# A third pair of exp blocks per unit on VectorE, in units 55 to 62 of a fused state-space and attention kernel

## The chip, the core and the metric

The kernel runs on one core of a Trainium2 chip. The metric is device time in microseconds from launch to end, as the median of several runs. TensorE is called PE below, VectorE DVE, ScalarE ACT, GpSimd POOL; SP is the engine whose queue issues the DMAs. PE multiplies matrices into PSUM (eight banks of 128 x 512 float32), the other engines read PSUM or on-chip memory (SBUF).

## The reference

From x (2048 tokens x 1024) two branches are computed and mixed by a gate of one number per token:

```python
g = sigmoid((x * gate_w).sum(-1, keepdims=True))
a = state_space(x)      # Bu = x B^T (complex), h_t = Lam_bar * h_{t-1} + Bu_t, y = 2 Re(h C^T) + x * Dskip
b = attention(x)        # 32 heads of 32: softmax(q k^T / sqrt(32)) v, then @ wo
out = g * a + (1 - g) * b
```

The attention needs 32 x 2048 x 2048 exponentials. They are what this text is about.

## The kernel before, in words

**Units and bursts.** The 32 heads are taken as 8 groups of 4 heads (`GROUPS`), the 2048 queries as 8 blocks of 256 (`QUNITS`). A group with a block of queries is a unit (0 to 63), and a unit is cut into 8 bursts (`BURSTS`), one for each 256 keys; burst p = 8U + i is burst i of unit U, and there are 512. In this text b0 to b7 are the bursts of a unit. A burst (`burst`, L1615) is 8 score matmuls (L1627, called QK here) into two of three PSUM slots of two banks, then two exponentials, one of each slot, by ACT into bfloat16 tiles: exp(0) at L1646, and exp(1) at L1646 or L1643. The slots rotate (`sl`), so the QK of burst p+1 needs the slot that exp(0) of burst p has read. It is issued as one operation that waits for both of its slots.

**Values.** `pv` (L1732) multiplies the exponentials with V into one PSUM bank (bank 6, token "O"). It runs one burst behind: at burst p it takes exp(1) of burst p-2 and exp(0) of burst p-1, at b1 only what is left of the unit before, at b2 six quarters of a burst at once. After b1 of the next unit the sum over keys is complete: `normalize` issues a reciprocal (L1745) and a multiplication (L1746) on DVE, and a transposing DMA on SP into `OT`.

**The blocks that DVE takes (x).** In chosen bursts ACT's exp(1) leaves out the last 256 of its 1024 columns (L1643 in place of L1646), and DVE and POOL compute these 256 by a polynomial. A pair of such blocks is a batch: two `x_in` (L1636, one in each of the two bursts) scale the scores out of PSUM into integers `xi` (two buffers, by the batch's parity). Then three DVE operations on the 512 columns of both (`x_q`: L1670, L1671, L1667) and one of POOL (`x_p`, L1668) follow, and four small matmuls (`x_pv`, L1711, pvx here) add the batch's values to bank 6. exp(1) of such a burst has an explicit dependence on its `x_in`. There is one `xq` (float32, written by the DVE steps, read by POOL) and one `xp` (bfloat16, written by POOL, read by pvx). So a batch's first `x_q` waits until POOL has read the last batch's `xq`, and POOL waits until the pvx of the last batch is through.

```python
        return [(0.61, DEP, lambda: self.dve(... lo, E2 / E3 * w, lo, ...), i2, ["xq"], "x_q")),      # L1670
                (0.61, DEP, lambda: self.dve(... xq[:], E1 / E3 * w * w, lo, ...), ["xq"] + i2, ["xq"], "x_q")),   # L1671
                (X_LAST, DEP, last)]       # last(): x_q at L1667 on DVE, then x_p at L1668 on POOL
```

**Which bursts.** `X_PLAN` lists half units; in units 55 to 62 both halves are in it, so `X_AT` gives the pairs (b0, b2) and (b4, b6). `x_plan` notes when the values of a batch are taken: at b7 of the unit if the second burst is below 4, else at burst 9, which is b1 of the next unit.

**The order of the work is planned when the program is built.** `build` walks through the bursts with a clock of its own for DVE (`dve_t`) and for the burst (`t0`, advanced by `period`: 1.83, or 1.66 where the burst before has a narrowed exp). In each burst it issues QK, `x_in` (0.40 on its clock, not before t0 + 0.45), exp(0), then `values()` (pv, pvx, exp(1)), the normalization where one is due (0.62 from t0 + 0.86), matmuls of other work ("dense" chains in bank 7, four of 512 columns a burst), and then as much DVE work as fits before `limit`: `period` + 0.86 for a burst in which no chain ends, plus 0.25 before a burst with a normalization; 1.41 + 0.35 where a chain ends and the dense part was put ahead of the values ("behind"); `period` + 0.10 where it ends without that. An `x_q` costs 0.61 (the last 0.615) and 0.12 more (`DEP`) when it follows another x step. Where a chain ends, its evacuation from bank 7 by DVE (0.65 on the clock) is issued after that. The last `x_q` of a batch may not be issued before the pvx of the batch before it. If a batch isn't finished when its values are due, `values()` issues the rest first (`x_flush`). Engines run their queues in order, so this order is what they execute, however long things take.

**Other work in units 55 to 62.** The dense chains are output products (`d_out`, L1538): from unit 55's sixth burst on to burst 511 each takes two bursts, four matmuls in the even burst, four (three in units 55 to 57) in the odd one, and DVE evacuates it at the end of the odd burst with one operation (L1550); unit 55 begins with projections (L1429, evacuated at L1436). The even burst's four matmuls need bank 7 evacuated. Four chains of units 56 and 57 also leave two small DVE steps (L1556, L1557) after two of them.

Of the kernel before, what the change touches and what calls it, by code (L numbers as in the profile page):

```python
# [934 lines left out]

X_AT = ((0, 2), (4, 6), (0, 4))
X_PLAN = (64, 72, 80, 84, 88, 92, 96, 100, 104, 108, 112, 116, 120, 124, 128, 132, 136, 144, 152, 156, 160, 164, 168, 172, 176, 180, 184, 188, 192, 200, 208, 216, 220, 224, 228, 232, 236, 240, 244, 248, 252, 256, 260, 264, 268, 272, 276, 280, 284, 288, 292, 296, 300, 304, 308, 312, 316, 320, 324, 328, 332, 336, 344, 348, 352, 356, 360, 364, 368, 372, 376, 380, 384, 388, 392, 396, 400, 404, 408, 412, 416, 420, 424, 428, 432, 436, 440, 444, 448, 452, 456, 460, 464, 468, 472, 476, 480, 484, 488, 492, 496, 500, 504)
X_COLS = 256
F_TS, F_ST = 1.32, 1.24
DEP = 0.12  # L940
# [22 lines left out]
class FastPath:  # L963

    def __init__(self, nc, S, es, d, flag):
# [27 lines left out]
        self.tq = T("tq", [128, 2, 512], BF)  # L993
        self.xi = T("xi", [128, 2, 2 * X_COLS], I32)
        self.xq = T("xq", [128, 2 * X_COLS], F32)
        self.xp = T("xp", [128, 2 * X_COLS], BF)
        self.ut = T("ut", [128, 2, 512], F32)
# [617 lines left out]
    def burst(self, B):  # L1615
# [17 lines left out]
        if mine is not None:  # L1633
            b, n = mine
            s = sl[1]
            first = self.dve(lambda e: e.tensor_scalar(self.xi[:, b % 2, X_COLS * n:X_COLS * (n + 1)], ps[:, 2 * s + 1, 512 - X_COLS:512], X_A, X_LO, ALU.mult, ALU.max),  # L1636
                             [("S", s)], [("xi", b % 2, n)], "x_in")
        def exp(z):
            s, p = sl[z], self.pt_of(B, z)
            self.pt_own[p] = (B, z)  # L1640
            if z == 1 and first is not None:
                flat = lambda ap: ap.rearrange("p h n -> p (h n)")[:, 0:1024 - X_COLS]
                self.S.op("act", lambda e: e.activation(flat(self.tile[p]), flat(ps[:, 2 * s:2 * s + 2, :]), ACT.Exp, scale=SCALE),  # L1643
# [3 lines left out]
        exp(0)  # L1647
        return lambda: exp(1)

    def x_plan(self, U, pair):  # L1650
        self.x_when.setdefault(8 * U + (7 if pair[1] < 4 else 9), []).append(len(self.x_batch))
        for n, i in enumerate(pair):
            self.x_of[8 * U + i] = (len(self.x_batch), n)
        self.x_batch.append([8 * U + i for i in pair])
# [44 lines left out]
    def x_pv(self, b):  # L1699
# [3 lines left out]
        for n, B in enumerate(self.x_batch[b]):  # L1703
# [3 lines left out]
            def mm(e, n=n, i=i, g=g):  # L1707
                m = None
                for qt in range(2):
                    o = 33 * (4 * qt + 3)  # L1710
                    m = e.matmul(ps[:, 6, o:o + 33], self.xp[:, X_COLS * n + 128 * qt:X_COLS * n + 128 * (qt + 1)], V[:, g % 2, 2 * i + 1, 3, :],  # L1711
                                 start=False, stop=False, skip_group_check=True)
# [44 lines left out]
    def build(self):  # L1757
# [11 lines left out]
        self.plan()  # L1769
        self.pt_own = {}  # L1770
        self.x_of, self.x_batch, self.x_when = {}, [], {}
        self.xbg, self.x_done, self.x_out = [], set(), 0
        self.lane = ""
        self.opening()

# [38 lines left out]
        for p in range(first, NBURST):  # L1814
# [2 lines left out]
            self.p = p  # L1817
            if p > first:
                t0 += period
            if p % 4 == 0 and p in X_PLAN:  # L1820
                one = p % 8 == 0 and p + 4 not in X_PLAN and p < NBURST - 8
                self.x_plan(p // 8, X_AT[2 if one else p // 4 % 2])
            while p in self.x_of and self.x_of[p][1] == 0 and len(self.xbg) > 3:
# [3 lines left out]
            if p in self.x_of:  # L1827
                self.dve_t = max(self.dve_t, t0 + 0.45) + 0.4
                b, n = self.x_of[p]
                if n == 1:  # L1830
                    due = 8 * (p // 8) + (7 if p % 8 < 4 else 9)
                    self.xbg += [(c, d, f, due) for c, d, f in self.x_ops(b)]
                self.lane = "x"
            q0, q1 = self.quarters[p]
# [96 lines left out]
            while self.xbg or self.bg or self.bg2:  # L1931
                now = max(self.dve_t, t0 + 0.3)
                room = limit - now + 1e-9
                xs, bs = [], []
                for c, d, f, due in self.xbg:
                    if c == X_LAST and self.x_out != len(self.x_done):
                        break
                    xs.append((c, d))
                    if c == X_LAST:
                        break  # L1940
                for c, d, f, n in self.bg:
                    if not ((n in self.tabled or not self.bg2) and self.item_ready(n)) or sum(x[0] for x in bs) > room:
                        break
                    bs.append((c, d))
                ts = [(c, 0.0) for c, f in self.bg2[:8]]
                if not bs and not xs and not ts:
                    break
                best = None
                left = next((n for n, x in enumerate(self.xbg) if x[0] == X_LAST), 0) + 1
                soon = self.xbg and left > self.xbg[0][3] - p - X_LEFT  # L1950
                self.hurry = soon and self.xbg[0][3] - p <= 1
                for i in range(len(xs) + 1):
                    for j in range(len(bs) + 1):
                        if self.mixed(xs[:i], bs[:j], [])[0] > room:
                            break
                        for k in range(len(ts) + 1):
                            u, lead = self.mixed(xs[:i], bs[:j], ts[:k])
                            if u > room:
                                break
                            w = sum(x[0] for x in xs[:i] + bs[:j] + ts[:k])  # L1960
                            v = (w + ((0.3 if ended is not None else 9.0) if soon else X_SOON) * i + 0.05 * sum(x[0] for x in bs[:j]), i, j, k, lead)
                            if best is None or v > best:
                                best = v
                lead = best[4]
                if not lead:
                    break
                if lead == "x":
                    c, d, f, due = self.xbg.pop(0)
                elif lead == "b":
                    c, d, f, n = self.bg.pop(0)  # L1970
                else:
                    (c, f), d = self.bg2.pop(0), 0.0
                f()
                if c > 0:
                    self.dve_t = now + c + (d if self.lane == lead else 0.0)
                    self.lane = lead
# [185 lines left out]
```

## Time and profile before

| | us |
|---|---|
| median of 3 runs (lowest, highest) | 923.47 (923.18, 923.78) |
| the profiled execution's own time | 923.41 |
| its span, first to last instruction | 921.6 |
| ACT busy | 903.7 (98%) |
| PE busy | 881.4 (96%) |
| DVE busy | 769.4 (83%) |
| POOL busy | 101.9 (11%) |
| start of unit 55 to start of unit 63 in the span (QK of their b0) | 788.22 to 898.73 |

The profile page lists busy time by engine, the span in 40 slices, the chain of work that ended last, and groups of instructions by line. A busy PE is not a PE at its peak, because the ends of matmuls are modelled. Some matmul records are missing from the trace: of each chain of output products one is mostly not shown. In the timeline a row of "x3" is three instructions in a row on that engine; what stands in brackets is the engine's idle time before it and what ended it. An ACTIVATE's duration overlaps the next one, so the cost of one in a row of them is the distance between starts.

### The profile page before, as it was taken

The page shows a single profiled execution, that of the slowest core. Times are in us where ns is not written, and L with a number is a line of the kernel's source. Part 1 is how long each engine was busy: PE and PEld are TensorE (multiplying, and loading weights), DVE is VectorE, ACT ScalarE, POOL GpSimd, SP SyncE. Part 2 cuts the span into 40 slices and gives each one's busy share as a digit, 9 for nine tenths or more (in the row PEclk, how much of TensorE's full clock was granted, in tenths as well). Part 3 has the DMA queues.
Part 4 walks back from the last instruction along what each step waited for, and adds up shares of the span by engine and source line. Part 5 has one row for each costly group of instructions (what it writes and reads, how often), then busy time and mean ns, then how long its engine had stood idle before and what let it go on. Part 6 is the DMA issues. An engine that isn't in the chain of part 4 may idle for free.

```text
span 921.6 us, 33844 instructions
## 1 busy us (share of the span) xinstructions
PE 881.4 (96%) x15095; PEld 503.7 (55%) x15316; DVE 769.4 (83%) x1365; ACT 903.7 (98%) x1034; POOL 101.9 (11%) x167
## 2 busy tenths in 40 slices
PE   7899998999999999999999999999999999999996
PEld 4555744557545565556655565555655556545553
DVE  2778989999889999999999989999999655676665
ACT  6999999999999999999999999999999999999997
POOL 2000001102101111111111111011110101001000
PEclk9999999999999999999999999999999999999998
DMA  9549767740463202361022420612002114434322
GB/s 202 80 103 154 106 111 138 143 90 16 91 126 90 65 20 61 91 137 45 19 74 65 104 57 19 139 47 83 23 17 54 31 51 134 119 88 123 118 64 75
DMA packets 170983, 77.70 MB, mean 84 GB/s; under 512 B 147280, under 2 KB 155472, under 8 KB 170832
## 3 DMA queue, kind: packets, MB, share of 16 engines
q1 hardware_dynamic: 168672, 74.94, 35.7%
q8 instruction: 121, 1.98, 0.9%
q10 hardware_dynamic: 2160, 0.53, 0.3%
q14 instruction: 30, 0.25, 0.1%
HBM read 25.18 MB, written 20.97 MB: 50 GB/s over the span
## 4 chain that ended last, share of the span: by engine, by line
PE 52%; ACT 28%; DVE 14%; issue 2%; SPq 1%; DMA 1%; POOL 0%
ACT f_pt L1646 22%; PE f_ps L1732 12%; PE f_ps L1627 10%; PE f_ps L1429 8%; PE f_ps L1507 8%; PE f_ps L1460 7%; PE f_ps L1448 5%; ACT f_pt L1643 5%; DVE f_xi L1636 3%; DVE f_ht L1365 2%; SPq L1065 1%; ACT f_cT L1646 1%; DVE f_Ag L1520 1%; DVE f_ub L1464 1%; DVE f_xq L1670 1%
## 5 line engine op out<-in xcount | busy, mean ns | idle before, releaser
L1646 ACT ACTIVATE f_pt<-f_ps 128x1024 bf16<-128x1024 f32 x738 | 712.0, 1082 | 3.3 <-PE f_ps L1627 3.0
L1732 PEld LDWEIGHTS f_ps<-f_V,f_pt 128*128 128x128 bf16 x7140 | 221.7, 96 | 94.8 <-issue 66.3
L1732 PE MATMUL f_ps<-f_V,f_pt 128*128 128x33 bf16 x7140 | 256.9, 178 | 0.1
L1627 PE MATMUL f_ps<-f_Q,f_K 32*128 32x256 bf16 x4096 | 203.6, 273 | 10.5 <-ACT f_pt L1646 2.9
L1643 ACT ACTIVATE f_pt<-f_ps 128x768 bf16<-128x768 f32 x206 | 183.2, 889 | 0.0
L1668 POOL TENSOR_SCALAR f_xp<-f_xq 128x512 int16<-128x512 f32 x103 | 82.8, 804 | 598.7 <-DVE f_xq L1667 423.8
L1627 PEld LDWEIGHTS f_ps<-f_Q,f_K 32*128 32x128 bf16 x4096 | 60.8, 92 | 144.4 <-ACT f_pt L1646 117.6
L1460 PE MATMUL f_ps<-f_xT,f_wb 128*128 128x512 bf16 x448 | 117.7, 379 | 8.9 <-DVE f_ub L1464 1.8
L1429 PE MATMUL f_ps<-f_xT,f_wb 128*128 128x512 bf16 x406 | 106.7, 379 | 4.1 <-issue 0.4
L1636 DVE TENSOR_SCALAR f_xi<-f_ps 128x256 int32<-128x256 f32 x206 | 86.8, 421 | 25.8 <-PE f_ps L1627 21.6
L1365 DVE TENSOR_TENSOR_SCAN f_ht<-f_pf,f_init,f_ut 128x512 bf16<-128x512 f32 x64 | 81.1, 1275 | 0.0
L1671 DVE SCALAR_TENSOR_TENSOR f_xq<-f_xq,f_xi 128x512 f32<-128x512 f32 x103 | 71.0, 689 | 2.5
L1670 DVE SCALAR_TENSOR_TENSOR f_xq<-f_xi 128x512 f32<-128x512 uint16 x103 | 70.7, 686 | 2.5 <-POOL f_xp L1668 0.7
L1667 DVE SCALAR_TENSOR_TENSOR f_xq<-f_xi,f_xq 128x512 f32<-128x512 int16 x103 | 70.9, 688 | 1.9
L1507 PE MATMUL f_ps<-f_cT,f_hp 128*128 128x512 bf16 x240 | 67.6, 379 | 2.5 <-DVE f_Ag L1520 0.6
L1460 PEld LDWEIGHTS f_ps<-f_xT,f_wb 128*128 128x128 bf16 x512 | 40.1, 96 | 41.4 <-issue 10.2
L1448 PE MATMUL f_ps<-f_wb,f_xT 128*128 128x128 bf16 x896 | 59.3, 219 | 0.0
L1429 PEld LDWEIGHTS f_ps<-f_xT,f_wb 128*128 128x128 bf16 x464 | 36.1, 96 | 35.3 <-issue 7.6
L1448 PEld LDWEIGHTS f_ps<-f_wb,f_xT 128*128 128x128 bf16 x896 | 50.4, 97 | 3.8 <-issue 3.8
L1464 DVE CAST f_ub<-f_ps 128x512 bf16<-128x512 f32 x64 | 44.0, 687 | 7.8 <-PE f_ps L1460 6.9
L1745 DVE RECIPROCAL f_rc<-f_ps 128x8 f32<-128x8 f32 x63 | 13.0, 206 | 40.6 <-PE f_ps L1711 36.2
L1356 DVE TENSOR_TENSOR f_ut<-f_ht,f_tq 128x512 f32<-128x512 bf16 x64 | 43.0, 691 | 0.6
(149 smaller groups left out, 816.6 us busy)
## 6 DMA issues: line engine op xcount, KB each, us to landing
u_scratch<-f_ub SPq DMA_DIRECT2D x64, 128.0 KB, 1.9
f_ub<-u_scratch SPq DMA_DIRECT2D x32, 256.0 KB, 2.9
ag_scratch<-f_Ag SPq DMA_DIRECT2D x32, 256.0 KB, 2.0
f_hp<-ag_scratch SPq DMA_DIRECT2D x32, 256.0 KB, 3.1
f_wb<-in_B_wqkv_dram SPq DMA_DIRECT2D x21, 256.0 KB, 4.0
out_dram<-f_xT SPq DMA_DIRECT2D x16, 256.0 KB, 2.0
f_cT<-in_B_wo_dram SPq DMA_DIRECT2D x5, 256.0 KB, 6.6
f_OT<-f_On SPq DMA_TRANSPOSE x63, 2.5
```

Of the source, the lines that this page charges most:

```text
L1365: ops.append((1.2, 0.0, lambda ri=ri: dve(lambda e: e.tensor_tensor_scan(ht[:, ri, :], rr, ut[:, ri, :], self.init[:, ri, j:j + 1], ALU.mu ...
L1429: mms.append((1, lambda e, f, l, a=a, w=w: e.matmul(ps[:, bank, :], w[:, a, :], xT[:, a, 512 * ch:512 * (ch + 1)], start=f, stop=l), [tok] ...
L1448: m = e.matmul(ps[:, bank, 128 * q:128 * (q + 1)], xT[:, a, 128 * kt:128 * (kt + 1)], w[:, a, :], start=(a == 0), stop=(a == 7))
L1460: mms.append((1, lambda e, f, l, a=a: e.matmul(ps[:, 7, :], bT[:, (2 * n + ri) % 3, a, :], xT[:, a, 512 * ch:512 * (ch + 1)], start=f, sto ...
L1507: mms.append((1, lambda e, f, l, j=j, ri=ri, h=h: e.matmul(ps[:, 7, :], h[:, cols], cT[ri][:, j, 512 * cb:512 * (cb + 1)], start=f, stop=l ...
L1627: m = e.matmul(ps[:, 2 * sl[h // 2] + h % 2, 256 * kl:256 * (kl + 1)], K[32 * h:32 * h + 32, g % 2, 128 * kt:128 * (kt + 1)], Q[32 * h:32 ...
L1636: first = self.dve(lambda e: e.tensor_scalar(self.xi[:, b % 2, X_COLS * n:X_COLS * (n + 1)], ps[:, 2 * s + 1, 512 - X_COLS:512], X_A, X_LO ...
L1643: self.S.op("act", lambda e: e.activation(flat(self.tile[p]), flat(ps[:, 2 * s:2 * s + 2, :]), ACT.Exp, scale=SCALE), reads=[("S", s)], wr ...
L1646: self.act(lambda e: e.activation(self.tile[p], ps[:, 2 * s:2 * s + 2, :], ACT.Exp, scale=SCALE), [("S", s)], [("pt", p)], "exp")
L1668: self.pool(lambda e: e.tensor_scalar(bits, xq[:], X_K, 128.0 * (E0 + 126.0), ALU.mult, ALU.add), ["xq"], p2, "x_p")
L1670: return [(0.61, DEP, lambda: self.dve(lambda e: e.scalar_tensor_tensor(xq[:], lo, E2 / E3 * w, lo, ALU.add, ALU.mult), i2, ["xq"], "x_q") ...
L1732: m = e.matmul(ps[:, 6, o:o + 33], self.tile[p][:, h2, 256 * kl + 128 * qt:256 * kl + 128 * (qt + 1)], V[:, g % 2, 2 * i + kl, h, :], star ...
```

## The change

In units 55 to 62 (`X_THREE`) VectorE takes three pairs instead of two: (b0, b1) with its values at b5, (b2, b4) with its values at b7, (b5, b6) with its values at burst 9, that is b1 of the next unit. So six of the eight exp(1) of a unit are narrowed instead of four: b0, b1, b2, b4, b5, b6. `x_plan` takes the due burst as an argument, and `x_due` keeps it for each batch. One more edit: the planning loop for DVE stops when no room is left before `limit`, also where something is still queued.

```diff
+X_THREE = (55, 56, 57, 58, 59, 60, 61, 62)
+X_THREE_AT = (((0, 1), 5), ((2, 4), 7), ((5, 6), 9))
...
-    def x_plan(self, U, pair):
-        self.x_when.setdefault(8 * U + (7 if pair[1] < 4 else 9), []).append(len(self.x_batch))
+    def x_plan(self, U, pair, due=None):
+        due = due or (7 if pair[1] < 4 else 9)
+        self.x_when.setdefault(8 * U + due, []).append(len(self.x_batch))
+        self.x_due.append(8 * U + due)
...
-            if p % 4 == 0 and p in X_PLAN:
+            if p // 8 in X_THREE:
+                for pair, due in X_THREE_AT if p % 8 == 0 else ():
+                    self.x_plan(p // 8, pair, due)
+            elif p % 4 == 0 and p in X_PLAN:
...
-                    due = 8 * (p // 8) + (7 if p % 8 < 4 else 9)
+                    due = self.x_due[b]
...
-                if not bs and not xs and not ts:
+                if room <= 0.0 or not bs and not xs and not ts:
                     break
```

More of the change, by code (lines that the diff above doesn't have):

```diff
@@ L1771, in build @@
         self.x_of, self.x_batch, self.x_when = {}, [], {}
-        self.xbg, self.x_done, self.x_out = [], set(), 0
+        self.xbg, self.x_done, self.x_out, self.x_due = [], set(), 0, []
         self.lane = ""
```

## The prediction

> **What bounds the kernel now.** I read the page's busy shares and slices first, then the chain that ended last in units 55 to 62, then the busy time of each unit, then one unit instruction by instruction.
>
> ```profile
> PE 881.4 (96%) x15095; PEld 503.7 (55%) x15316; DVE 769.4 (83%) x1365; ACT 903.7 (98%) x1034; POOL 101.9 (11%) x167
> DVE  2778989999889999999999989999999655676665
> L1646 ACT ACTIVATE f_pt<-f_ps 128x1024 bf16<-128x1024 f32 x738 | 712.0, 1082 | 3.3 <-PE f_ps L1627 3.0
> ```
>
> ACT has next to no idle time, and DVE drops to 5 to 7 tenths in the last nine of the 40 slices; units 55 to 62 lie in the last six. The chain in order of time there is ACT alone:
>
> ```profile
> 849.24 2.75 ACT f_pt L1646 x3
> 851.99 0.70 ACT f_pt L1643
> 852.69 2.75 ACT f_pt L1646 x3
> ```
>
> So a wide exp costs 2.75 / 3 = 0.917 and a narrow one 0.70. A unit of 12 wide and 4 narrow ones is 13.80. The busy time by unit (columns: stretch, its length, then busy us of PE, PEld, DVE, ACT, POOL) agrees:
>
> ```profile
> core 0: us, PE busy (x) PEld busy (x) DVE busy (x) ACT busy (x) POOL busy (x), PEclk, DMA share, GB/s
> 843.48:857.29 13.81, 13.49 (x223) 7.10 (x225) 9.30 (x21) 13.81 (x17) 1.23 (x2) 1.00 0.37 122
> sum 110.51, PE 106.78 PEld 55.94 DVE 75.77 ACT 110.51 POOL 9.88; mean PE 13.35 PEld 6.99 DVE 9.47 ACT 13.81 POOL 1.23
> ```
>
> ACT is busy all the time, PE is close behind at full clock (1.00), DVE has 4.5 of 13.8 free. The cadence of PE, ACT and DVE over b7, b0, b1, b2 of one such unit:
>
> ```profile
> 841.68 0.40 PE L1627 MATMUL f_ps<-f_Q,f_K 32*128 32x256 bf16 x8
> 843.29 0.26 PE L1711 MATMUL f_ps<-f_V,f_xp 128*128 128x33 bf16 x4
> 843.48 0.40 PE L1627 MATMUL f_ps<-f_Q,f_K 32*128 32x256 bf16 x8
> 843.81 0.52 PE L1732 MATMUL f_ps<-f_V,f_pt 128*128 128x33 bf16 x14
> 845.13 0.40 PE L1627 MATMUL f_ps<-f_Q,f_K 32*128 32x256 bf16 x8
> 845.58 2.95 ACT L1646 ACTIVATE f_pt<-f_ps 128x1024 bf16<-128x1024 f32 x3
> 845.68 0.26 PE L1711 MATMUL f_ps<-f_V,f_xp 128*128 128x33 bf16 x4
> 845.97 0.21 DVE L1745 RECIPROCAL f_rc<-f_ps 128x8 f32<-128x8 f32 x1 [1.62 <-PE f_ps L1711]
> 846.75 0.40 PE L1627 MATMUL f_ps<-f_Q,f_K 32*128 32x256 bf16 x8
> 846.85 0.75 DVE L1550 SCALAR_TENSOR_TENSOR f_xT<-f_ps,f_gcol,f_hp 128x512 bf16<-128x512 f32 x1 [0.21 <-PE f_ps L1538]
> 847.52 0.42 DVE L1636 TENSOR_SCALAR f_xi<-f_ps 128x256 int32<-128x256 f32 x1
> 847.98 0.69 DVE L1670 SCALAR_TENSOR_TENSOR f_xq<-f_xi 128x512 f32<-128x512 uint16 x1
> 848.32 0.38 PE L1538 MATMUL f_ps<-f_wb,f_OT 128*128 128x512 bf16 x1
> 848.63 0.40 PE L1627 MATMUL f_ps<-f_Q,f_K 32*128 32x256 bf16 x8
> 848.70 0.69 DVE L1671 SCALAR_TENSOR_TENSOR f_xq<-f_xq,f_xi 128x512 f32<-128x512 f32 x1
> 849.40 0.59 PE L1538 MATMUL f_ps<-f_cT,f_OT 128*128 128x512 bf16 x2
> 849.43 0.69 DVE L1667 SCALAR_TENSOR_TENSOR f_xq<-f_xi,f_xq 128x512 f32<-128x512 int16 x1
> 849.84 0.56 PE L1732 MATMUL f_ps<-f_V,f_pt 128*128 128x33 bf16 x16
> 850.04 0.75 DVE L1550 SCALAR_TENSOR_TENSOR f_xT<-f_ps,f_gcol,f_hp 128x512 bf16<-128x512 f32 x1
> ```
>
> To be seen: exp(0) starts 0.45 after its QK (845.13, 845.58), and the next QK 1.17 after that exp(0) (846.75). A narrow burst can thus be 0.917 + 0.70 = 1.62 long at the least, exactly what QK to QK allows (0.45 + 1.17). PE itself needs 1.80 in b7 with its pvx (841.68 to 843.48, where it waited for nothing). In b2, with 22 pv matmuls, its last dense matmul starts at 848.32, so PE is free 1.78 after its QK at 0.2 a matmul (two take 849.40 to 849.84). In an even burst the 14 pv matmuls start 0.33 after QK (843.81) and are issued by about 0.70, where the dense ones follow; in an odd burst of full chains the evacuation comes 1.41 after QK (848.63, 850.04). A dependent x step follows the one before by 0.725, an evacuation follows it by 0.61, an `x_in` the evacuation by 0.67.
>
> **The change part by part.** *Gain.* 16 wide exps become narrow: 16 x 0.217 = 3.5 if nothing else binds; a unit would be 10 x 0.917 + 6 x 0.70 = 13.37.
>
> *PE.* The values only move: a narrowed block takes two matmuls out of pv, and pvx does two. But one pvx group now lies in b5, which becomes as full as b7 (1.80), and b5 is now narrow (1.62): 0.18 lost. b2 was 1.83 long behind a wide exp(1); behind a narrow one ACT wants it in 1.62 and PE needs 1.78: 0.16 lost. Unless DVE binds, a unit of full chains is then 13.71, 0.1 below before.
>
> *DVE and POOL.* Per unit two `x_in`, three `x_q`, one `x_p` more: 2 x 0.42 + 3 x 0.69 = 2.9 of DVE, which with 9.3 makes 12.2 of 13.4. That fits as a sum; the order decides. I work the order out by the planner's own constants (times within the burst; A, B, C are the batches due at b5, b7, b9). b1: `x_in` until 0.85, normalization 1.48, limit 1.76, nothing fits; evacuation until 2.41. b2 (1.66 later): `x_in` until 1.15, room 1.37, A1 fits (0.73), two don't (1.46). b3: from 0.30, limit 1.76, room 1.46; A2 with A3 needs 1.465, so A2 alone. b4: `x_in` until 0.85, A3 1.585, B1 2.315 (limit 2.69; B3 must wait for b5's pvx). b5: `x_in` 0.885, B2 1.615, evacuation. b6: `x_in` 1.005, B3 1.74, C1 2.47 (limit 2.52). b7: C2 1.54, evacuation. b0: `x_in` 0.93, C3. It closes on itself. The same arithmetic for before gives two x steps behind `x_in` in b2, one and the evacuation in b3, which is what the rows show.
>
> So B1 stands right behind A3, and C1 right behind B3. The planner's clock counts 0.73 for that. But `xq` is one buffer, and B1 can't start before POOL has read A3's. Before, this met once:
>
> ```profile
> 435.41 0.68 DVE L1667 SCALAR_TENSOR_TENSOR f_xq<-f_xi,f_xq 128x512 f32<-128x512 int16 x1
> 436.18 0.62 POOL L1668 TENSOR_SCALAR f_xp<-f_xq 128x512 int16<-128x512 f32 x1 [11.00 <-DVE f_xq L1667]
> 436.83 0.69 DVE L1670 SCALAR_TENSOR_TENSOR f_xq<-f_xi 128x512 f32<-128x512 uint16 x1 [0.74 <-POOL f_xp L1668]
> 439.86 1.53 POOL L1668 TENSOR_SCALAR f_xp<-f_xq 128x512 int16<-128x512 f32 x1 [3.07 <-DVE f_xq L1667]
> 441.44 0.27 PE L1711 MATMUL f_ps<-f_V,f_xp 128*128 128x33 bf16 x4 [0.84 <-POOL f_xp L1668]
> 443.00 1.02 ACT L1646 ACTIVATE f_pt<-f_ps 128x1024 bf16<-128x1024 f32 x1 [0.70 <-PE f_ps L1627]
> ```
>
> A first x step starts 1.42 after the third of the batch before, where a step without a dependence could follow after 0.61 to 0.69: 0.74 of DVE lost here, 0.80 at the spacing of 0.61, now twice a unit. The last rows show the second way to lose: pvx in b1 waited 0.84 for POOL, and ACT stood 0.70 behind the QK that followed. Behind each DVE delay stand, in its queue, the next `x_in` (for which exp(1) waits), the evacuation (for which the even burst's dense matmuls wait) and C3 with POOL and b1's pvx.
>
> *The chain of one steady unit,* with these durations in that order (times from each burst's QK; 0.05 assumed from `x_in` to ACT). b4: `x_in`, A3 at 0.85, wait 0.80, B1 at 2.27. b5: `x_in` only at 1.07, done 1.49, where exp(1) could start at 1.37: ACT loses 0.17. B2 at 1.42, evacuation at 2.04 instead of 1.41. b6: `x_in` at 0.96, ACT loses 0.07; dense starts at 0.96 instead of 0.70, the next QK is late, 0.14. B3 at 1.31, wait 0.80, C1 at 2.73. b7: C2 at 1.64, evacuation at 2.26 instead of 1.41. b0: `x_in` at 1.24, ACT loses 0.24; dense late, 0.14; C3 at 1.59, POOL until 2.98. b1: pvx 0.44 late, so evacuation, dense and QK of b2 too: 0.26. b2: `x_in` 0.03, the 22 pv matmuls 0.14. Sum 1.19: the unit is 13.37 + 1.19 = 14.56, 0.75 longer than before. In units 55 to 57 odd bursts have one matmul less, and the same working gives 14.31, 0.49 longer; unit 55 starts without a backlog, 0.1. Sum: 5 x 0.75 + 2 x 0.49 + 0.1 = 4.8.
>
> *Two small steps* (L1556, L1557) after two chains of units 56 and 57:
>
> ```profile
> L1557 DVE TENSOR_TENSOR f_Et<-f_Et 128x512 bf16<-128x512 f32 x2 | 1.4, 682 | 0.0
> L1556 DVE CAST f_Et<-f_Et 128x512 bf16<-128x512 f32 x2 | 0.8, 418 | 0.0
> ```
>
> They cost nothing before, as DVE was idle there. Bounds: 0 (they fall into the waits for POOL) and 2.2 (all shown); I take 0.5, near the lower end, since C2 and the evacuation have some room in those lighter units.
>
> *Bounds of the working.* The link from `x_in` to exp(1) never shows as a wait before, so its 0.05 is taken like the other links. The steps' spacing is bounded by 0.61 (taken where steps don't depend on each other) and the 0.69 of their duration, by which the 4.8 becomes 6.4. Without any wait for POOL the same working gives -1.3. The result is steep: it crosses zero where DVE waits 0.58 instead of 0.80. No DMA is added; normalizations and output stores shift by some tenths, their readers are a burst or more away. The edit of the loop and `x_due` cost nothing, being done at build time.
>
> *A rule.* The page shows the POOL step's mean:
>
> ```profile
> L1668 POOL TENSOR_SCALAR f_xp<-f_xq 128x512 int16<-128x512 f32 x103 | 82.8, 804 | 598.7 <-DVE f_xq L1667 423.8
> ```
>
> 0.80 against 0.62 when alone, and 1.53 at 439.86. In the worked order DVE itself waits during A's and B's step, and C's meets `x_in`, so I keep 0.62. The Trainium skill (SBUF — State Buffer, Who interferes with whom) says that a DVE instruction with two SBUF inputs and a GpSimd instruction that reads SBUF block each other, the later one for the whole instruction; by it the step would be 0.62 only while no `x_q` runs, and the 1.53 agrees with it.
>
> The sum is 923.41 (profiled; the median is 0.06 above) + 4.8 + 0.5 = 928.7.
>
> **The rivals.** *Not slower: the waits on POOL don't show,* because some step stands between A3 and B1 and between B3 and C1, or because the delays fall into DVE's 1.6 us wait before the reciprocal (845.97). It decides at a wait of 0.58. For it: DVE's sum fits. Against: the planner's arithmetic reproduces the old order. Then PE's limits in b2 and b5 leave 5 x 0.1 and 3 x 0.27, that is -1.3 and 922.1. *The full gain:* in addition PE isn't the limit in b2 and b5, since a record of each chain is missing and I may have placed the dense matmuls too late: -3.5 and 919.9. *Heavier:* POOL's step takes its mean of 0.80, as x steps run beside it: the same chain gives +8.8 and 932.2. This is what the skill's rule would do if steps collide. *PE bound throughout* would cancel the gain: 923.4, with the first rival's sign undecided.
>
> **How the numbers follow.** Forecast (926 to 931.5 its own range) 0.60; heavier 0.08; waits hidden or PE bound 0.18; full gain or most of it 0.14. A measurement of this kernel tells 0.2%, 1.85 us. So faster 0.14, same 0.18, slower 0.68. The range from 921.0 to 932.5 takes in the first rival and the heavier one, and leaves out most of the full gain.
>
> **What would show it.** Right: DVE idle some 0.7 in front of L1670, released by L1668, about 16 times; ACT idle before L1643 by `x_in` (L1636) at b5, b6, b0; PE waiting for L1668 before pvx in b1; a unit of 14.3 to 14.6. Wrong: units of 13.4 to 13.7 with ACT unbroken, or L1670 without a wait.

## The result, and the profile after

The changed kernel took 928.27 us (median; 927.73 to 929.12) beside 923.18 for the kernel before: 1.0052 times as long, with an interval of 1.0042 to 1.0063, that is 3.9 to 5.8 us slower. The profiled execution took 927.73, its span 926.0. Line numbers have moved: the wide exp is L1648, the narrow one L1645, QK L1629, `x_in` L1638, the three `x_q` L1674, L1675 and L1671, POOL's `x_p` L1672, pvx L1715, pv L1736, the evacuation L1552.

The page, lines of its busy times, slices and groups:

```profile
PE 902.6 (97%) x15316; PEld 505.5 (55%) x15316; DVE 786.0 (85%) x1405; ACT 904.3 (98%) x1034; POOL 107.0 (12%) x175
...
DVE  2788989999989999999899889999999556787776
...
L1648 ACT ACTIVATE f_pt<-f_ps 128x1024 bf16<-128x1024 f32 x722 | 696.8, 1072 | 8.7 <-PE f_ps L1629 8.2
...
L1674 DVE SCALAR_TENSOR_TENSOR f_xq<-f_xi 128x512 f32<-128x512 uint16 x111 | 76.0, 685 | 13.7 <-POOL f_xp L1672 12.5
```

16 exps have become narrow (738 wide ones before, 722 now), and DVE is fuller in the last slices, but nowhere full. The last line shows the loss: before a batch's first `x_q` DVE stood 12.5 us for POOL, in the whole program. The waits of units 55 to 62 (us in total, times, longest):

```profile
DVE f_xq L1674 <- POOL f_xp L1672: 11.8, 16, 0.7
...
ACT f_pt L1648 <- PE f_ps L1629: 5.2, 23, 0.4
...
PEld f_ps L1715 <- POOL f_xp L1672: 0.9, 2, 0.4
```

Sixteen waits, two a unit, of 0.73 to 0.74 each. To compare units I take the distance between the rows of eight pv matmuls in b1, one row a unit, from that of unit 55 to that of unit 63. As windows, of before and then of after (columns as in the prediction: length; busy us of PE, PEld, DVE, ACT, POOL; clock; DMA), the eight units together:

```profile
790.21:900.72 110.51, 106.78 (x1757) 55.94 (x1785) 75.83 (x158) 110.51 (x129) 9.88 (x16) 1.00 0.31 93
```

```profile
789.50:906.09 116.59, 111.73 (x1788) 57.60 (x1785) 92.57 (x198) 111.24 (x129) 15.30 (x24) 1.00 0.29 87
```

They are 6.1 longer, and ACT is idle for 5.4 of them, where it was busy throughout. (PE's busy time counts 31 matmuls more that were not recorded before.) One steady unit after, PE, DVE, ACT and POOL from b2 to the next b2, in order of time (rows that the argument does not need are left out):

```profile
849.26 0.40 PE L1629 MATMUL f_ps<-f_Q,f_K 32*128 32x256 bf16 x8
850.63 0.81 ACT L1645 ACTIVATE f_pt<-f_ps 128x768 bf16<-128x768 f32 x1
851.15 0.40 PE L1629 MATMUL f_ps<-f_Q,f_K 32*128 32x256 bf16 x8
851.60 2.86 ACT L1648 ACTIVATE f_pt<-f_ps 128x1024 bf16<-128x1024 f32 x3 [0.17 <-PE f_ps L1629]
...
853.58 0.68 DVE L1671 SCALAR_TENSOR_TENSOR f_xq<-f_xi,f_xq 128x512 f32<-128x512 int16 x1
854.35 0.62 POOL L1672 TENSOR_SCALAR f_xp<-f_xq 128x512 int16<-128x512 f32 x1 [6.22 <-DVE f_xq L1671]
855.00 0.69 DVE L1674 SCALAR_TENSOR_TENSOR f_xq<-f_xi 128x512 f32<-128x512 uint16 x1 [0.74 <-POOL f_xp L1672]
855.02 1.06 ACT L1648 ACTIVATE f_pt<-f_ps 128x1024 bf16<-128x1024 f32 x1
855.61 0.42 DVE L1638 TENSOR_SCALAR f_xi<-f_ps 128x256 int32<-128x256 f32 x1
856.06 0.81 ACT L1645 ACTIVATE f_pt<-f_ps 128x768 bf16<-128x768 f32 x1
856.31 0.40 PE L1629 MATMUL f_ps<-f_Q,f_K 32*128 32x256 bf16 x8
856.54 0.74 DVE L1552 SCALAR_TENSOR_TENSOR f_xT<-f_ps,f_gcol,f_hp 128x512 bf16<-128x512 f32 x1
857.35 0.82 PE L1540 MATMUL f_ps<-f_cT,f_OT 128*128 128x512 bf16 x3 [0.20 <-DVE f_xT L1552]
857.68 0.81 ACT L1645 ACTIVATE f_pt<-f_ps 128x768 bf16<-128x768 f32 x1
858.32 0.40 PE L1629 MATMUL f_ps<-f_Q,f_K 32*128 32x256 bf16 x8
858.77 2.85 ACT L1648 ACTIVATE f_pt<-f_ps 128x1024 bf16<-128x1024 f32 x3 [0.29 <-PE f_ps L1629]
858.96 0.69 DVE L1674 SCALAR_TENSOR_TENSOR f_xq<-f_xi 128x512 f32<-128x512 uint16 x1 [0.73 <-POOL f_xp L1672]
...
861.11 0.82 PE L1540 MATMUL f_ps<-f_cT,f_OT 128*128 128x512 bf16 x3 [0.20 <-DVE f_xT L1552]
861.50 0.83 ACT L1645 ACTIVATE f_pt<-f_ps 128x768 bf16<-128x768 f32 x1
862.07 0.62 POOL L1672 TENSOR_SCALAR f_xp<-f_xq 128x512 int16<-128x512 f32 x1 [3.14 <-DVE f_xq L1671]
862.53 1.02 ACT L1648 ACTIVATE f_pt<-f_ps 128x1024 bf16<-128x1024 f32 x1 [0.20 <-PE f_ps L1629]
862.75 0.27 PE L1715 MATMUL f_ps<-f_V,f_xp 128*128 128x33 bf16 x4
863.45 0.81 ACT L1645 ACTIVATE f_pt<-f_ps 128x768 bf16<-128x768 f32 x1
863.82 0.40 PE L1629 MATMUL f_ps<-f_Q,f_K 32*128 32x256 bf16 x8
864.27 1.02 ACT L1648 ACTIVATE f_pt<-f_ps 128x1024 bf16<-128x1024 f32 x1
```

From b2's QK to the next b2's are 14.56 (849.26 to 863.82). Where ACT loses it is seen in the distances of its starts, 0.92 after a wide exp and 0.70 after a narrow one when nothing holds it. Follow the first wait: `x_q` stands 0.74 at 855.00; so b5's `x_in` comes at 855.61, is done at 856.03, and the narrow exp behind it starts 1.04 after its wide one instead of 0.92. The evacuation behind both comes at 856.54, b6's dense matmuls wait for it until 857.35, the QK behind them is issued at 858.32, two us after the one before, and the wide exp that needs it starts 1.09 after a narrow one instead of 0.70.

### The profile page after: what moved, and what is told of

The parts are those of the page before. It is cut to its first block, busy times and chain, and to the rows that moved or that the text cites. A ratio compares the mean times of both kernels' runs of the same rounds, so it can differ in the third digit from the quotient of the medians.

```text
span 926.0 us, 34097 instructions
## 1 busy us (share of the span) xinstructions
PE 902.6 (97%) x15316; PEld 505.5 (55%) x15316; DVE 786.0 (85%) x1405; ACT 904.3 (98%) x1034; POOL 107.0 (12%) x175
## 4 chain that ended last, share of the span: by engine, by line
PE 71%; ACT 14%; DVE 9%; POOL 2%; issue 1%; SPq 1%; DMA 1%
PE f_ps L1736 18%; PE f_ps L1629 14%; PE f_ps L1431 11%; ACT f_pt L1648 10%; PE f_ps L1509 10%; PE f_ps L1462 8%; PE f_ps L1450 5%; PE f_ps L1540 3%; POOL f_xp L1672 2%; DVE f_xq L1671 2%; DVE f_xT L1552 1%; DVE f_xq L1674 1%; ACT f_pt L1645 1%; PE f_ps L1715 1%; SPq L1067 1%
## 5 line engine op out<-in xcount | busy, mean ns | idle before, releaser
L1648 ACT ACTIVATE f_pt<-f_ps 128x1024 bf16<-128x1024 f32 x722 | 696.8, 1072 | 8.7 <-PE f_ps L1629 8.2
L1736 PEld LDWEIGHTS f_ps<-f_V,f_pt 128*128 128x128 bf16 x7108 | 221.0, 96 | 94.7 <-issue 65.7
L1736 PE MATMUL f_ps<-f_V,f_pt 128*128 128x33 bf16 x7108 | 256.1, 178 | 0.0
L1629 PE MATMUL f_ps<-f_Q,f_K 32*128 32x256 bf16 x4096 | 203.3, 273 | 8.8 <-ACT f_cT L1648 2.4
L1645 ACT ACTIVATE f_pt<-f_ps 128x768 bf16<-128x768 f32 x222 | 193.2, 870 | 0.0
L1672 POOL TENSOR_SCALAR f_xp<-f_xq 128x512 int16<-128x512 f32 x111 | 88.5, 797 | 599.5 <-DVE f_xq L1671 477.6
L1629 PEld LDWEIGHTS f_ps<-f_Q,f_K 32*128 32x128 bf16 x4096 | 60.7, 92 | 142.3 <-ACT f_pt L1648 111.2
L1462 PE MATMUL f_ps<-f_xT,f_wb 128*128 128x512 bf16 x512 | 131.5, 378 | 2.3 <-DVE f_ub L1466 1.6
L1431 PE MATMUL f_ps<-f_xT,f_wb 128*128 128x512 bf16 x464 | 119.3, 379 | 0.0
L1638 DVE TENSOR_SCALAR f_xi<-f_ps 128x256 int32<-128x256 f32 x222 | 93.2, 420 | 28.8 <-PE f_ps L1629 25.8
L1674 DVE SCALAR_TENSOR_TENSOR f_xq<-f_xi 128x512 f32<-128x512 uint16 x111 | 76.0, 685 | 13.7 <-POOL f_xp L1672 12.5
L1675 DVE SCALAR_TENSOR_TENSOR f_xq<-f_xq,f_xi 128x512 f32<-128x512 f32 x111 | 76.4, 688 | 2.5
L1671 DVE SCALAR_TENSOR_TENSOR f_xq<-f_xi,f_xq 128x512 f32<-128x512 int16 x111 | 76.0, 685 | 1.4
L1509 PE MATMUL f_ps<-f_cT,f_hp 128*128 128x512 bf16 x272 | 74.6, 379 | 0.1
L1540 PE MATMUL f_ps<-f_cT,f_OT 128*128 128x512 bf16 x156 | 45.1, 381 | 3.9 <-DVE f_xT L1552 2.9
```

What stands on the lines that cost most here:

```text
L1431: mms.append((1, lambda e, f, l, a=a, w=w: e.matmul(ps[:, bank, :], w[:, a, :], xT[:, a, 512 * ch:512 * (ch + 1)], start=f, stop=l), [tok] ...
L1462: mms.append((1, lambda e, f, l, a=a: e.matmul(ps[:, 7, :], bT[:, (2 * n + ri) % 3, a, :], xT[:, a, 512 * ch:512 * (ch + 1)], start=f, sto ...
L1509: mms.append((1, lambda e, f, l, j=j, ri=ri, h=h: e.matmul(ps[:, 7, :], h[:, cols], cT[ri][:, j, 512 * cb:512 * (cb + 1)], start=f, stop=l ...
L1629: m = e.matmul(ps[:, 2 * sl[h // 2] + h % 2, 256 * kl:256 * (kl + 1)], K[32 * h:32 * h + 32, g % 2, 128 * kt:128 * (kt + 1)], Q[32 * h:32 ...
L1648: self.act(lambda e: e.activation(self.tile[p], ps[:, 2 * s:2 * s + 2, :], ACT.Exp, scale=SCALE), [("S", s)], [("pt", p)], "exp")
L1671: self.dve(lambda e: e.scalar_tensor_tensor(xq[:], hi, 128.0 / X_K, xq[:], ALU.mult, ALU.add), i2 + ["xq"], ["xq"], "x_q")
```

## The experiments

In two kernels of the list below PE's work is lighter; they and their control leave heads out, as their expectations say. The unit lengths of all kernels, from the rows named above:

| us, unit | 55 | 56 | 57 | 58 | 59 to 62 | all eight |
|---|---|---|---|---|---|---|
| before | 13.81 | 13.82 | 13.81 | 13.81 | 13.81 to 13.82 | 110.51 |
| after | 14.38 | 14.42 | 14.61 | 14.94 | 14.55 to 14.57 | 116.59 |
| second xq | 13.52 | 13.57 | 14.00 | 14.13 | 13.74 to 13.75 | 110.20 |
| POOL's step twice | 15.78 | 17.85 | 16.71 | 17.04 | 16.66, 17.96, 16.67, 16.66 | 135.33 |
| after, lighter PE | 14.37 | 14.42 | 14.39 | 14.39 | 14.00 to 14.02 | 113.61 |
| second xq, lighter PE | 13.52 | 13.57 | 13.85 | 13.38 | 13.38 to 13.39 | 107.87 |
| before, lighter PE | 13.81 | 13.81 | 13.82 | 13.81 | 13.81 to 13.82 | 110.50 |
| second xq, other bursts | 13.46 | 13.44 | 14.27 | 15.38 | 14.41, 13.68, 13.68, 13.69 | 112.01 |
| one xq, other bursts | 13.66 | 13.75 | 14.21 | 15.54 | 14.67, 13.95, 13.94, 13.95 | 113.67 |
| second xq, small steps on POOL | 13.52 | 14.47 | 13.72 | 13.74 | 13.74 to 13.75 | 110.44 |
| second xq, other bursts, small steps on POOL | 13.45 | 14.22 | 14.06 | 13.69 | 13.68 to 13.69 | 110.16 |

**A second xq.** Every other batch of units 55 to 62 takes another buffer in place of `xq`, so no first `x_q` has to wait until POOL has read the batch before. Order and work stay the same.

```diff
+        kq = "xq"
+        if self.x_batch[b][0] // 8 in X_THREE and b % 2:
+            xq, kq = self.ut[:, 0, :], ("ut", 0)
...
-        return [(0.61, DEP, lambda: self.dve(... i2, ["xq"], "x_q")),
+        return [(0.61, DEP, lambda: self.dve(... i2, [kq], "x_q")),
```

> The changed kernel, but in units 55 to 62 every second batch uses another buffer in place of xq (the first half of ut, free by then), so a batch's first x_q no longer waits for POOL to read the batch before; order and amount of work are the same. If the wait on xq is what costs (my theory), no wait of the first x_q on POOL is left, and the chain worked for a unit gives 13.54 in units 55 to 57 and 13.72 after: -1.3 us against the kernel before, about 922, so 6 us below the changed kernel. If DVE is simply too full with nine x steps a unit, the time stays 3 us or more above before. If PE is the bound, it changes by less than 1.5 us from the changed kernel's +5. If ACT alone binds once the wait is gone, -3.5 us.

Measured: 922.17, 0.9988 times before (0.9979 to 0.9997). A row for L1677, the first `x_q` here, waiting for POOL no longer exists. Its timeline (DVE and POOL; L1674 is the third `x_q` here, L1678 the second, L1675 POOL's step):

```profile
864.89 0.68 DVE L1674 SCALAR_TENSOR_TENSOR f_ut<-f_xi,f_ut 128x512 f32<-128x512 int16 x1
865.49 0.69 DVE L1677 SCALAR_TENSOR_TENSOR f_xq<-f_xi 128x512 f32<-128x512 uint16 x1
865.66 1.00 POOL L1675 TENSOR_SCALAR f_xp<-f_ut 128x512 int16<-128x512 f32 x1 [6.22 <-DVE f_ut L1674]
...
869.17 0.99 POOL L1675 TENSOR_SCALAR f_xp<-f_xq 128x512 int16<-128x512 f32 x1 [2.52 <-DVE f_xq L1674]
869.72 0.98 DVE L1678 SCALAR_TENSOR_TENSOR f_ut<-f_ut,f_xi 128x512 f32<-128x512 f32 x1
```

The next batch's first step starts 0.60 after the third one instead of 1.42, and the eight units are 6.4 shorter than after (110.20 for 116.59). That the single buffer causes the loss is thereby shown. What the wait kept apart now meets: POOL's step, begun while an `x_q` runs, takes 1.00 for 0.62, and an `x_q` begun while POOL's step runs takes 0.98 for 0.69. Neither reaches ACT: in a steady unit the distances of its starts are more than 0.02 longer than 0.92 and 0.70 only in b2 (by 0.27) and in b5 (by 0.13), the two bursts in which the prediction had PE as the limit. The Trainium skill (SBUF — State Buffer, Who interferes with whom) states that a DVE instruction with two SBUF inputs contends with a GpSimd instruction that reads SBUF; by these rows it does.

**POOL's step twice.** One `xq`, and in the eight units POOL issues its step a second time.

```diff
+            if self.x_batch[b][0] // 8 in X_THREE:
+                self.pool(lambda e: e.tensor_scalar(bits, xq[:], X_K, ...), ["xq"], p2, "x_p")
```

> The changed kernel with the POOL step of each batch in units 55 to 62 issued twice (the second one writes the same values again), which doubles the time until xq is read: 1.24 instead of 0.62. If the waits on POOL set the length of the unit (my theory), the worked chain gives units of 16.2 to 16.5 and +19 us against before, that is 14 more than the changed kernel. If the waits only fill time in which DVE or ACT would stand still anyway, it costs less than 3 us more than the changed kernel.

Measured: 949.91, 1.0279 times before (1.0259 to 1.0298), 26.4 us. Waits of the eight units, and one of two units that are longer than the others as windows show it:

```profile
DVE f_xq L1676 <- POOL f_xp L1674: 23.0, 16, 1.4
...
ACT f_pt L1645 <- DVE f_xi L1638: 9.4, 16, 0.7
```

```profile
874.71:892.67 17.96, 14.76 (x224) 7.54 (x224) 11.37 (x25) 14.02 (x16) 3.70 (x7) 0.91 0.31 93
```

Each wait is 1.44 for 0.74, and a steady unit 16.66 for 14.56, 2.1 more. The two waits on `xq` give 1.40 of it. The rest is a third wait, which this kernel lengthens too: pvx in b1 also waits for POOL's second step.

```profile
910.37 0.27 PE L1717 MATMUL f_ps<-f_V,f_xp 128*128 128x33 bf16 x4 [0.67 <-POOL f_xp L1674]
```

It starts 1.03 after the pv before it (909.34), where in after it starts 0.34 after (862.41 to 862.75), and the narrow exp of b1 to the next wide one takes 1.52 for 0.82. So 0.70, 0.70 and 0.69 more of waiting are 2.1 more of the unit: each further delay reaches ACT in full. The run doubles the waits on `xq` and this one together, and doesn't price the waits on `xq` alone.

The steady unit is within 0.2 of what was expected; the sum was missed by more: the eight units are 24.8 longer than before, 2.5 of it because units 56 and 60 ran at a granted clock of 0.90 and 0.91 (their neighbours 1.00) and took 1.2 and 1.3 longer than a steady one. In each of the two the clock was 0.50 for 3.4 us (from 807.7 and from 876.0) and 1.00 otherwise; a third such stretch, from 927.1, lies behind the eight units. Why the clock fell there and not in the neighbours, which have the same waits, stays open.

**Lighter PE, with one xq and with two.** From burst 460 on the output products take three dense matmuls a burst for four.

```diff
-        js = dict(full=range(8), part=range(7), rest=[7])
+        js = dict(full=range(6), part=range(7), rest=[7])
...
-            quota = MM_PER_PERIOD
+            quota = 3 if p >= 460 else MM_PER_PERIOD
```

> The changed kernel with its one xq, but from burst 460 on the output chains leave out two of their eight matmuls (heads of the last two groups are missing in those outputs) and run three a burst instead of four, which takes 0.2 us of PE from every burst. If the waits on xq cost (my theory), they are all still there and most of the loss stays: the worked chain gives +2.6 us against before (units of 14.16 instead of 14.57; evacuations come earlier and PE catches up faster). If PE is the bound, the loss is gone and the gain shows: -2 to -3.5 us.

> Both: the second buffer for xq and the lighter output chains from burst 460 on (heads of the last two groups missing in those outputs). If the two PE limits I named (the 22 pv matmuls of b2, and b5 with its pvx) hold back the second-buffer kernel, they are gone here, and units 58 to 62 fall from 13.72 to 13.39: -3.0 us against before, 1.7 below the kernel with the second buffer alone. If PE doesn't limit there, this run equals the one with the second buffer alone.

Measured: with one `xq` 925.51, 1.0020 (1.0011 to 1.0029); with two 920.10, 0.9961 (0.9947 to 0.9975). The eight units of each:

```profile
790.23:903.84 113.61, 97.79 (x1711) 53.21 (x1740) 92.84 (x198) 111.05 (x129) 15.08 (x24) 1.00 0.30 89
```

```profile
791.70:899.57 107.87, 98.71 (x1711) 51.72 (x1740) 94.76 (x198) 107.51 (x129) 21.62 (x24) 1.00 0.31 95
```

With PE light and one `xq` the 16 waits are all there, and a steady unit is 14.01 (14.16 expected), still longer than the 13.81 of before, which the lighter PE leaves as it is (next run). But only 0.20 of the 0.75 is left, less than the "most of the loss" that was expected. (Units 55 and 56 lie ahead of burst 460 and are as in after.) With a second `xq` and PE light the unit is 13.39, the 13.37 of ACT alone, so PE is what keeps the second `xq` at 13.75. Against that 13.37 PE's load alone costs a steady unit 0.38, the waits alone 0.64, and both together 1.19 (14.56). The gain that the change aims at is had only where both limits go.

**Control: the kernel before with the same lighter PE.**

> The kernel before with the output chains from burst 460 on cut to six matmuls, three a burst (heads of the last two groups missing in those outputs). If ACT alone sets the pace of the kernel before in these units, nothing is gained there (units of 13.81): within 0.5 us of before. If PE bound it already, it gets 1 us or more faster.

Measured: 922.50, 0.9987 (0.9978 to 0.9996).

```profile
791.69:902.19 110.50, 99.02 (x1711) 51.41 (x1740) 75.80 (x158) 110.50 (x129) 9.88 (x16) 1.00 0.32 93
```

The units are as long as before, so ACT alone bounds them there. The ratio is nevertheless below 1 by 0.13%, more than the 0.5 us expected. It would have to come from outside these units, and no trace here shows where: the profiled execution of this run took 923.73 for 923.41. A ratio of that size says nothing of the units: for the second `xq` (0.9988) the units' own 0.3 us is the better number.

**Other bursts with a second xq.** b3 is narrowed in place of b2, which holds 22 pv matmuls, and the first pair's values move to b6, so that b5 has no pvx.

```diff
-X_THREE_AT = (((0, 1), 5), ((2, 4), 7), ((5, 6), 9))
+X_THREE_AT = (((0, 1), 6), ((3, 4), 7), ((5, 6), 9))
```

> The second buffer for xq, all work in place, but the three pairs are (b0, b1), (b3, b4), (b5, b6) with values at b6, b7 and b9: b2 with its 22 pv matmuls stays wide, and no pvx lies in b5. If the two PE limits are as I worked them out, no narrow burst is longer than 1.64 now, a unit takes 13.43, and the kernel is 3.1 us below before (about 920.1). If PE limits the sum of a unit and not single bursts, it equals the second-buffer kernel with the old pairs (-1.3). If the waits on xq were not the cause, it is slower than before like the changed kernel.

Measured: 923.92, 1.0005 (0.9996 to 1.0014), a miss. The steady units are 13.68 for the 13.43 hoped for, and 57 to 59 are much longer. Unit 58's start, DVE, POOL, PE and ACT (here L1718 is pvx):

```profile
831.71 0.68 DVE L1674 SCALAR_TENSOR_TENSOR f_xq<-f_xi,f_xq 128x512 f32<-128x512 int16 x1
832.47 0.62 POOL L1675 TENSOR_SCALAR f_xp<-f_xq 128x512 int16<-128x512 f32 x1 [3.47 <-DVE f_xq L1674]
833.14 0.27 PE L1718 MATMUL f_ps<-f_V,f_xp 128*128 128x33 bf16 x4 [1.54 <-POOL f_xp L1675]
...
834.67 2.91 ACT L1648 ACTIVATE f_pt<-f_ps 128x1024 bf16<-128x1024 f32 x3 [1.59 <-PE f_ps L1629]
```

The last batch of unit 57 has all its `x_q` a burst later than in a steady unit, its values come due before POOL has them, and PE and then ACT stand 1.5 us. What pushed it back are the two small steps on DVE: with them on POOL, in the run below, unit 58 takes 13.69 for 15.38. The steady units miss 13.43 because PE itself makes two narrow bursts longer than 1.62: b4 with 16 pv matmuls takes 1.71 from QK to QK (879.55 to 881.26 in this run), and b6, which now holds the pvx taken from b5, 1.75 (882.90 to 884.65).

**The small steps on POOL,** with a second `xq`, on the bursts of the change and on the other bursts:

```diff
-                    self.bg2 += [(0.34, lambda: self.dve(lambda e: e.tensor_copy(hi, su), ...)),
-                                 (0.72, lambda: self.dve(lambda e: e.tensor_tensor(lo, su, hi, ALU.subtract), ...))]
+                    self.pool(lambda e: e.tensor_copy(hi, su), [("sum7", i)], [("hi", i)])
+                    self.pool(lambda e: e.tensor_tensor(lo, su, hi, ALU.subtract), [("sum7", i), ("hi", i)], [("lo", i)])
```

> The second buffer for xq, and the four small steps of the last output chains (L1556, L1557 of the kernel before) are done by POOL instead of DVE; all work in place. In the second-buffer kernel units 57 and 58 took 14.00 and 14.13 where 13.55 and 13.74 stand around them; if the small steps are the reason, both fall into line: 0.8 us below the second-buffer kernel, about -2.0 against before. If those units are long because the chains change from seven to eight matmuls there, nothing changes.

> Second buffer, small steps on POOL, and the pairs (b0, b1), (b3, b4), (b5, b6) with values at b6, b7, b9; all work in place. With the old place of the small steps this choice of pairs lost 0.5 to 1.6 us in each of units 57 to 59, and its other units took 13.45 (55, 56) and 13.68 (60 to 62). If the small steps upset the planned order there, all units are 13.45 or 13.68 now: -1.8 us against before, some 0.5 below the run with the old pairs and small steps on POOL. If single bursts bound PE as I first worked it out (13.43), it would be -3.

Measured: 922.58, 0.9988 (0.9979 to 0.9997), and 922.33, 0.9984 (0.9975 to 0.9993). Both miss most of the gain hoped for: their eight units are 0.1 and 0.35 shorter than before. In the first, units 57 and 58 fall into line (13.72 and 13.74 for 14.00 and 14.13), so the small steps were their excess; but unit 56 goes from 13.57 to 14.47. There, in the kernel with the change's own bursts (POOL, DVE, ACT):

```profile
813.36 1.48 POOL L1559 TENSOR_TENSOR f_Et<-f_Et 128x512 bf16<-128x512 f32 x1
813.75 1.64 DVE L1677 SCALAR_TENSOR_TENSOR f_ut<-f_xi 128x512 f32<-128x512 uint16 x1
814.92 0.95 POOL L1675 TENSOR_SCALAR f_xp<-f_xq 128x512 int16<-128x512 f32 x1
815.42 0.98 DVE L1678 SCALAR_TENSOR_TENSOR f_ut<-f_ut,f_xi 128x512 f32<-128x512 f32 x1
...
816.58 1.02 ACT L1648 ACTIVATE f_pt<-f_ps 128x1024 bf16<-128x1024 f32 x1 [0.40 <-PE f_ps L1629]
```

The steps now hold up `x_q` from beside it (1.64 for 0.69), and POOL's own step behind them in its queue. The cost has moved, not gone.

**Other bursts with one xq.** The same pairs with the single buffer: in units 60 to 62 only one first `x_q` stands right behind a third one instead of two.

> The changed kernel with its one xq, only the pairs are (b0, b1), (b3, b4), (b5, b6) with values at b6, b7, b9. In the planned order of units 60 to 62 a first x_q now stands right behind a third one once a unit (in b6) instead of twice; in b4 the evacuation and an x_in stand between. If each wait on xq has its price, these units lie between the two-wait kernel (14.56) and the same pairs without a wait (13.68): the worked chain, with 0.1 us more of PE in even bursts than I took, gives 13.99. If one wait a unit still fits into DVE's free time, they are 13.7. In all, with the disturbed units 57 to 59, 1 to 3 us above before.

Measured: 925.89, 1.0027 (1.0017 to 1.0037). The wait in the eight units:

```profile
DVE f_xq L1674 <- POOL f_xp L1672: 5.9, 8, 0.7
```

Half the waits, and a steady unit is 13.95 where it is 13.68 with a second `xq`: 0.27 for one wait, against 0.81 (14.56 less 13.75) for two on the change's bursts. The expected unit was 13.99.

None of the kernels that do all the work is clearly ahead of the kernel before: the best ratio, 0.9984, lies inside the control's interval (0.9978 to 0.9996), and the best eight units are 110.16 for 110.51.

## Why the prediction was right

The forecast was 928.7, slower, and the median is 928.27. By its own steps:

*The order and the waits: right.* The order worked out by hand is the one in the rows, B1 right behind A3 and C1 right behind B3, and DVE stood 0.73 to 0.74 there 16 times (0.74 and 0.80 taken). POOL's step took 0.62 in 22 of the 24 batches, so the heavier rival did not occur.

*The steady unit: right in its sum, less so in its places.* 14.56 forecast, 14.56 measured. ACT's losses, from the distances of its starts in the rows of after less 0.92 or 0.70:

| lost in | forecast | measured |
|---|---|---|
| b5, `x_in` late | 0.17 | 0.12 (856.06 less 855.02, less 0.92) |
| b6, and its dense matmuls late | 0.21 | 0.39 (858.77 less 857.68) |
| b0, and its dense matmuls late | 0.38 | 0.33 (862.53 less 861.50) |
| b1, pvx late | 0.26 | 0.12 (864.27 less 863.45) |
| b2, 22 pv matmuls | 0.17 | 0.27 (851.60 less 850.63) |

The sums are 1.19 and 1.23. One of the marks named in advance failed: `x_in` held ACT only in b5, not in b6 and b0, where the late evacuation alone did it. Another held, but smaller: the list of waits has PE waiting for POOL before pvx in two units only (0.4 each), yet in b1 of each steady unit pvx starts 0.05 after POOL's end (862.07 + 0.62, 862.75) and 0.34 after its pv, where before it was 0.22 (845.46 to 845.68). The 0.12 is what ACT loses in b1. It doesn't show as idle time, because the pv matmuls still count as busy (862.41 to 862.78).

That the sum fits is luck: the terms of `x_in` were forecast at 0.51 and are 0.12, the others at 0.68 and are 1.11, and the two errors cancelled. PE needs 1.89 in b2 (849.26 to 851.15) and not 1.78: from the start of its last dense matmul to the next QK the prediction took 0.2, and its own rows have 0.31 (848.32 to 848.63), as in after (850.84 to 851.15). In b6 the dense matmuls start 1.04 after QK (856.31 to 857.35) and not 0.96.

*Units 55 to 57: too small.* The forecast was 0.1 longer for unit 55 and 0.49 each for units 56 and 57; measured are 0.57 and 0.60 in units 55 and 56, and about as much in unit 57 beside its small step. The 0.1 was set without a working. Unit 55 has both waits like the others, and in the distances of ACT's starts it loses 0.12 in b5, 0.39 in b6 and 0.32 in the b0 behind it. *The small steps* were taken at 0.5 and cost about 0.6: unit 57 is 0.2 above unit 56, unit 58 is 0.4 above unit 59. They do it through POOL: beside the second of them (L1559, 0.68 on DVE) POOL's step takes 0.99 and 1.00, and these are the two b1 in which pvx waits 0.4.

*The sum.* The eight units are 6.1 longer, the forecast was 5.3; the term that was mis-sized most is that of unit 55 (0.1 for 0.57). The whole profiled execution is 4.3 longer: the stretch up to unit 55's row is 0.7 shorter, that from unit 63's row to the end 1.0 (20.88 before, 19.91 after). Neither is of the change. The kernels of all runs reach unit 55's row, ahead of all waits on `xq` in these units, at 789.5 to 791.7. At the end, the time from unit 63's row to the last instruction on DVE is 16.7 in both, so the 1.0 lies behind that instruction; the other kernels took 19.7 to 20.0 for that whole stretch, the control with before's own exps too (POOL's step twice, with its low clock there, 22.5). The medians differ by 5.1, between the units' 6.1 and the profiled executions' 4.3, so it is by luck that the forecast of 5.3 is nearer to the time than its units were to theirs.

*Without the waits* the forecast was 922.1 and the kernel with a second `xq` took 922.17, which is luck again: its units give 0.3 of the 1.3 forecast, and the control shows a ratio as low with no shorter unit. PE in b2 (0.27 lost for 0.16, which makes the unit 13.75 for 13.71) and the small steps in units 57 and 58 (14.00 and 14.13) take the rest, terms that the rival left out or set too low. *The full gain* needs PE free: it came only with heads left out (13.39). *The stop where no room is left* adds no instruction; its effect by itself was not tried.

## What to carry to other kernels

A scratch buffer that one engine fills and another empties is a lock between them: when a planner sets two batches back to back, count the reader's whole step and both hand-overs (here 1.42 from start to start, for 0.61), or give each other batch a buffer of its own. Work that fits an engine's free time as a sum (12.2 of 13.4 us here) can still slow the kernel, because everything queued behind a wait, the input step and the evacuation here, moves with it. Where two engines are within a few per cent of each other, relieving the one buys little until the other is relieved as well; a control with the second one's load cut shows how much is behind it.

## What the runs showed of the hardware that was not expected

Contention between DVE and POOL can be read as an order. An `x_q` begun during POOL's step ends 0.54 after that step's end (870.70 against 870.16 with the second `xq`; 815.39 against 814.84 beside the 1.48 us step), whatever it had already waited; alone it takes 0.69. POOL's step begun during an `x_q` ends 0.48 after it (866.66 against 866.18); alone it takes 0.62. So the later one stands until the earlier is nearly through. This is what the Trainium skill (SBUF — State Buffer, Who interferes with whom) says of the shared ports, an exclusive lock. The wait in the changed kernel had hidden it, as POOL's step was alone there in 22 of 24 batches. The 1.53 us step in which the prediction saw it stood beside a scan on DVE with two inputs (L1365, 439.69, 1.28 us long), not beside an `x_q`; it ends 0.42 after the scan.
